# The first expert product as seven half-size products on half chunks of 256 columns, with the sums of the tokens kept

## The chip, the cores and the metric

The kernel runs on one core of a Trainium2 chip. The metric is the device time of one execution in microseconds. The core has engines that run side by side, each with its own queue in program order: TensorE (PE, matrix products into PSUM banks), VectorE (DVE) and ScalarE (ACT), which read PSUM, GpSimd (POOL), which here works in SBUF, and SyncE (SP), which issues the transfers.

## The reference

Three layers in float32: attention with a sink and a window, a dense mixture of eight experts, and a feed-forward layer.

```
x = attention(q, k, v)                       # 1536 tokens x 512
P = exp(x @ w_gate - max)                    # 1536 x 8 experts
for _ in range(8):
    P /= P.sum(1) + 1e-9;  P /= P.sum(0) + 1e-9;  P *= N / E
out = sum over e of P[:, e] * (relu(x @ w1[e]) @ w2[e])     # 512 -> 1024 -> 512
y = relu(out @ w_in) ** 2 @ w_out            # 512 -> 2048 -> 512
```

## The kernel before

Every float32 operand is split into a high and a low part (`xh` and `xl`, `wh` and `wl`), both in the rounded format that the matmuls read, and a product is three matmuls: high by low, high by high, low by high. The depth of 512 is four slices of 128.

The experts' hidden columns are cut into chunks of 512: chunks 0 to 15 are the eight experts (two each), chunks 16 to 19 the feed-forward layer. Chunk 0 fills TensorE's gaps in the attention phase (`phase_a`), with 384 tokens to a matmul. From chunk 1 on (`phase_b`) a chunk is taken for three blocks of 512 tokens. For each block come four groups of the first product (`mm1`, L452: 12 matmuls, weights stationary, 512 tokens as columns), each followed by a relu into `hh` on ScalarE (L464) and by the low part `hl` on VectorE (L465); then the four groups of the second product (`mm2`, L500) of the block before, one for each 128 tokens, each followed by an accumulation in `acc` on VectorE, scaled with the expert's column of P (L518; L513 and L515 without a scale). An engine's order is the order of the code: `phase_b` records a group, then its evacuation, then one step of the side work.

Side work is the splitting of the next chunk's weights (high part on ScalarE L390, low part on GpSimd L391), and the gate, a generator of half steps. A half step normalises P by rows (four small VectorE operations, L582 to L585) or by columns (a matmul with ones on TensorE, L590, and four operations, L594 to L600). The weights of the feed-forward layer come as 64-bit floats and are converted by eight VectorE operations per piece of 512 (L401 to L424, in four steps); 8 pieces of a chunk are spread over the 24 groups of the chunk before, one step to a group. Ahead of chunk 16 the accumulated tokens are transposed back (`x2`: L528 on TensorE, `xh` on ScalarE L534, `xl` on VectorE L535).

Of the kernel before, what the change touches and what calls it, by code (L numbers as in the profile page):

```python
# [19 lines left out]
NT = B * S  # L20
# [14 lines left out]
QKW = (QW + KW[0], QW + KW[1])  # L35
BIG = 1e30
# [3 lines left out]
class Kernel:  # L40
# [8 lines left out]
    def pool(self, ctx, name, bufs=1, space=None):  # L49
        if space:  # L50
            return ctx.enter_context(self.tc.tile_pool(name=name, bufs=bufs, space=space))
        return ctx.enter_context(self.tc.tile_pool(name=name, bufs=bufs))
# [311 lines left out]
    def w_load(self, c, which, half=0):  # L364
        src = (self.w1, self.w2)[which][c]
        pool = self.wraw[self.wk % len(self.wraw)]
        self.wk += 1
        if c < NC1:
            raw = pool.tile([128, KD, FC], F32, tag="wraw", name="wraw")
        else:  # L370
            raw = pool.tile([128, KD // 2, FC, 2], I32, tag="wraw", name="wraw64")
            s = slice(half * KD // 2, (half + 1) * KD // 2)
            src = src[:, s].bitcast(I32).rearrange("p k (f t) -> p k f t", t=2)
        self.nc.sync.dma_start(out=raw, in_=src)
        self.wr[c, which, half] = raw

    def w_split(self, c, which, piece, n=4):

        nc = self.nc
        if piece == 0:  # L380
            pool = self.wp[c % 2]
            nm = f"w{which}_{c % 2}"
            self.W[c, which] = tuple(
                pool.tile([128, KD, FC], F32R, tag=nm + t, name=nm + t) for t in "hl"
            )
        hi, lo = self.W[c, which]
        s = slice(piece * KD // n, (piece + 1) * KD // n)
        if c < NC1:
            src = self.wr[c, which, 0][:, s]
            nc.scalar.activation(out=hi[:, s], in_=src, func=AF.Copy)  # L390
            nc.gpsimd.tensor_tensor(  # L391
                out=lo[:, s], in0=src, in1=hi.bitcast(F32)[:, s], op=ALU.subtract
            )
            return

        raw, k = self.wr[c, which, piece // 2], piece % 2
        h, l = raw[:, k, :, 1], raw.bitcast(U32)[:, k, :, 0]
        x, m = (self.rp.tile([128, FC], I32, tag=t, name=t) for t in ("cx", "cm"))
        sg = self.rp1.tile([128, FC], I32, tag="cs", name="cs")
# [7 lines left out]
            out=sg, in0=h, scalar1=-0x80000000, scalar2=None, op0=ALU.bitwise_and  # L407
# [10 lines left out]
            out=x, in0=x, scalar=23, in1=sg, op0=ALU.logical_shift_left, op1=ALU.bitwise_or  # L418
# [7 lines left out]
        nc.scalar.activation(out=hi[:, piece], in_=mf, func=AF.Copy)  # L426
        nc.gpsimd.tensor_tensor(
            out=lo[:, piece], in0=mf, in1=hi.bitcast(F32)[:, piece], op=ALU.subtract
        )
# [8 lines left out]
    def mm1(self, ps, c, t0, n, f):  # L438
        nc = self.nc
        if f == 0:  # L440
            pool = self.hp[0 if n == QW else self.hk % 2]
            self.hk += 1
            self.h[c, t0] = tuple(
                pool.tile([128, KD, 512], F32R, tag="h" + t, name="h" + t) for t in "hl"
            )
        w1h, w1l = self.W[c, 0]
# [12 lines left out]
    def mm1_evac(self, c, t0, n, f, ps):  # L459
# [9 lines left out]
        else:  # L469
            r = self.rp.tile([128, 512], F32, tag="r", name="r")  # L470
            gq = self.rp.tile([128, 512], F32, tag="gq", name="gq")
# [5 lines left out]
            self.late = gq, hh, hl, f  # L477

    def finish(self):

        if self.late:
            gq, hh, hl, f = self.late
            nc = self.nc
            nc.scalar.activation(out=hh[:, f, :], in_=gq, func=AF.Copy)
            nc.vector.tensor_tensor(
                out=hl[:, f, :], in0=gq, in1=hh.bitcast(F32)[:, f, :], op=ALU.subtract
            )
            self.late = None
# [18 lines left out]
    def mm2_evac(self, c, t0, n, t, ps):  # L507
        nc = self.nc
        ti = t0 // 128 + t
        a = self.acc[:, ti, :]  # L510
        self.finish()
        if c in (0, NC1):
            nc.vector.tensor_copy(out=a, in_=ps)  # L513
        elif c == 1 or c > NC1:
# [6 lines left out]
        if c == NC1 + NC2 - 1:  # L521
            nc.sync.dma_start(out=self.out[ti * 128 : (ti + 1) * 128, :], in_=a)
# [17 lines left out]
    def gate(self):  # L540
        nc, g = self.nc, self.gp
        pt = self.mmtile()
        for b in range(3):
# [7 lines left out]
            lg = self.rp.tile([16, 512], F32, tag="r", name="lg")  # L551
# [55 lines left out]
    def moe_groups(self, first):  # L607

        if first == 1:
            for t0 in range(0, NT, QW):  # L610
                for f in range(FC // 128):
                    yield ("1", 0, t0, QW, f)
                for t in range(QW // 128):
                    yield ("2", 0, t0, QW, t)
        blocks = [(c, t0, 512) for c in range(first, NC1 + NC2) for t0 in range(0, NT, 512)]
        for k, (c, t0, n) in enumerate(blocks):
            for f in range(FC // 128):
                yield ("1", c, t0, n, f)
            if blocks[k + 1 : k + 2] and blocks[k + 1][0] == NC1:
                for kc in range(KD):  # L620
                    yield ("x", c, *blocks[k + 1][1:], kc)
            if k:
                for t in range(4):
                    yield ("2", *blocks[k - 1], t)
        for t in range(4):
            yield ("2", *blocks[-1], t)

    def group(self, gr):

        kind, c, t0, n, i = gr  # L630
        if kind == "x":
            self.x2(t0 // 512, i)
            return
# [11 lines left out]
    def filler(self, gen):  # L645

        for gr in gen:
            if gr[1] > 0:
                self.next = gr
                return  # L650
# [4 lines left out]
    def run(self):  # L655
# [17 lines left out]
        with ExitStack() as all_:  # L673
            self.reset()
            self.wp = [self.pool(all_, "wp0"), None]
            self.hp = [self.pool(all_, "hp0"), None]
            self.wraw = [self.pool(all_, "wraw0")]
            with tc.manual_schedule():
                gen = self.moe_groups(1)
                with ExitStack() as actx:  # L680
                    self.att = self.pool(actx, "att")
# [7 lines left out]
                    fill = self.phase_a(gen)  # L689
                self.phase_b(all_, 1, fill, gen)  # L690
        with tc.If(nc.values_load(self.flag, min_val=0, max_val=1)):
            with ExitStack() as all_:
                self.reset()
                with tc.manual_schedule():
# [5 lines left out]
                    self.wp = [self.pool(all_, "gwp0"), None]  # L700
                    self.hp = [self.pool(all_, "ghp0"), None]
                    self.wraw = [self.pool(all_, "gwraw0")]
                    gen = self.moe_groups(0)
                    self.phase_b(all_, 0, None, gen)

    def reset(self):
        self.mmk = self.hk = self.wk = 0
# [102 lines left out]
    def phase_a(self, gen):  # L810
# [27 lines left out]
        for u in range(U + 4):  # L838
# [35 lines left out]
            for i in [i for i, x in enumerate(W_AT) if x == u]:  # L874
                for _ in self.w_split(0, *divmod(i, 4)):
                    pass
# [4 lines left out]
    def phase_b(self, ctx, c0, fill, gen):  # L881
        nc = self.nc
        self.wp[1] = self.pool(ctx, f"wp1{c0}")
        self.wraw.append(self.pool(ctx, f"wraw1{c0}"))
        self.wk = 1
        self.hp[1] = self.pool(ctx, f"hp1{c0}")
        self.rp = self.pool(ctx, f"rp{c0}", 2)
        self.rp1 = self.pool(ctx, f"rp1{c0}")
# [3 lines left out]
        wg = self.pool(ctx, f"wg{c0}")  # L892
        self.wgz = wg.tile([128, KD, 128], F32R, name="wgz")
        wgr = wg.tile([128, KD, E], F32, name="wgr")
        nc.gpsimd.memset(self.wgz.bitcast(F32), 0.0)
        self.ones = wg.tile([128, 128], F32, name="ones")
        nc.gpsimd.memset(self.ones, 1.0)
        nc.sync.dma_start(out=wgr, in_=self.wg)
        events = {}
        loads = []  # L900
        for c in range(c0, NC1 + NC2):
            for which in range(2):
                for half in range(1 if c < NC1 else 2):
                    loads.append((c, which, half))
                for piece in range(4):
                    if c == 0:
                        at = (0, 0)
                    elif c == c0:
                        at = (which, piece)
                    else:  # L910
                        k = 4 * which + piece
                        at = (c - 1, {c0 + 1: 3 + 2 * k, NC1 + 1: 3 * k}.get(c, 1 + 3 * k))
                    events.setdefault(at, []).append(("split", c, which, piece))
        for piece in range(4):
            events.setdefault((2, 9 + piece), []).append(("scale", piece))
        loads.reverse()
        for _ in range(2):
            self.w_load(*loads.pop())
        h = self.wgz[:, :, 0:E]
# [131 lines left out]
```

## Time and profile before

| | before |
|---|---|
| median of 3 runs | 1485.55 us (1484.77 to 1487.75) |
| profiled execution: time, span | 1482.95 us, 1481.1 us |
| TensorE busy | 1448.7 us, 98% |
| VectorE busy | 679.6 us, 46% |
| ScalarE busy | 376.2 us, 25% |
| GpSimd busy | 278.5 us, 19% |
| mean granted clock of TensorE | 0.995 |

The time of an execution holds the span of the instructions and 1.85 us around it. A duration in a view is that of one instruction; neighbours on an engine can overlap a little, so the distance between two starts is what a queue pays.

### The profile page before, as it was taken

What the parts mean: (1) busy time and instruction counts of PE and PEld (TensorE: products, weight loads), DVE (VectorE), ACT (ScalarE), POOL (GpSimd) and SP (SyncE); (2) the same over time, 40 slices, a digit from 0 to 9 for tenths busy, and PEclk for the clock granted to TensorE, in tenths of its full rate; (3) what the DMA queues carried; (4) which work ended last, traced back from release to release, by engine and by line L of the source; (5) the groups of instructions that cost most, each with busy time, mean ns of one, the idle gap of its engine ahead of it and who ended that gap; (6) DMA issues with size and microseconds to landing.
All of it is one profiled execution on the core that took longest, in us unless ns stands there. A gap on an engine that the chain in (4) does not pass through costs nothing.

```text
span 1481.1 us, 16715 instructions
## 1 busy us (share of the span) xinstructions
PE 1448.7 (98%) x6791; PEld 1201.6 (81%) x6791; DVE 679.6 (46%) x1373; ACT 376.2 (25%) x807; POOL 278.5 (19%) x238
## 2 busy tenths in 40 slices
PE   5899999999999999999999999999999999999998
PEld 4688887888888888888888888888888888888887
DVE  7988836242222222222222222222223789688832
ACT  5767622111111211111121111112111133232221
POOL 4543312111111211111111111111110112011100
PEclk9899999999999999999999999999999999999999
DMA  3323121000001000000100000010000122011001
GB/s 111 116 61 94 35 86 57 29 29 29 29 29 58 29 29 29 29 29 29 58 29 29 29 29 29 29 58 27 30 29 29 57 86 84 30 58 58 29 22 66
DMA packets 15045, 67.76 MB, mean 46 GB/s; under 512 B 2160, under 2 KB 4208, under 8 KB 8816
## 3 DMA queue, kind: packets, MB, share of 16 engines
q1 hardware_dynamic: 14672, 66.61, 13.5%
q8 instruction: 55, 0.90, 0.3%
q14 instruction: 30, 0.25, 0.1%
q10 hardware_dynamic: 288, 0.00, 0.0%
HBM read 63.46 MB, written 3.15 MB: 45 GB/s over the span
## 4 chain that ended last, share of the span: by engine, by line
PE 93%; DVE 5%; ACT 1%; DMA 0%; issue 0%; ACTq 0%; DVEq 0%
PE mm L500 44%; PE mm L452 43%; PE xp L348 3%; PE sc L220 1%; DVE p L260 1%; PE ptp L273 1%; DVE p L233 1%; DVE st L250 1%; DMA wn_i<-window 0%; ACT qkh L175 0%; DVE ptl L309 0%; PE mm L547 0%; DVE hl L465 0%; ACT p L243 0%; PE mm L528 0%; DVE rs L583 0%
## 5 line engine op out<-in xcount | busy, mean ns | idle before, releaser
L464 ACT ACTIVATE hh<-mm 128x512 fp32r<-128x512 f32 (+1 forms) x196 | 115.3, 588 | 795.5 <-PE mm L452 795.5
L465 DVE SCALAR_TENSOR_TENSOR hl<-mm,hh 128x512 fp32r<-128x512 f32 (+1 forms) x196 | 133.3, 680 | 373.5 <-ACT hh L464 373.5
L518 DVE SCALAR_TENSOR_TENSOR acc<-mm,P,acc 128x512 f32<-128x512 f32 x168 | 125.9, 750 | 279.0 <-PE mm L500 279.0
L452 PE MATMUL mm<-xl,w_0h 128*128 128x512 f32 (+1 forms) x496 | 191.1, 385 | 0.0
L452 PE MATMUL mm<-xh,w_0h 128*128 128x512 f32 (+1 forms) x496 | 190.6, 384 | 0.0
L452 PE MATMUL mm<-xh,w_0l 128*128 128x512 f32 (+1 forms) x496 | 189.7, 382 | 0.0
L500 PE MATMUL mm<-w_0h,hh 128*128 128x512 f32 x480 | 187.7, 391 | 0.0
L500 PE MATMUL mm<-w_0l,hh 128*128 128x512 f32 x480 | 187.5, 391 | 0.0
L452 PE MATMUL mm<-xh,w_1l 128*128 128x512 f32 x480 | 187.2, 390 | 0.0
L500 PE MATMUL mm<-w_1h,hl 128*128 128x512 f32 x480 | 187.1, 390 | 0.0
L500 PE MATMUL mm<-w_0h,hl 128*128 128x512 f32 x480 | 186.9, 389 | 0.0
L452 PE MATMUL mm<-xh,w_1h 128*128 128x512 f32 x480 | 186.8, 389 | 0.0
L500 PE MATMUL mm<-w_1l,hh 128*128 128x512 f32 x480 | 186.8, 389 | 0.0
L500 PE MATMUL mm<-w_1h,hh 128*128 128x512 f32 x480 | 186.7, 389 | 0.0
L452 PE MATMUL mm<-xl,w_1h 128*128 128x512 f32 x480 | 186.7, 389 | 0.0
L391 POOL TENSOR_TENSOR w_1l<-wraw,w_1h 128x512 fp32r<-128x512 f32 x64 | 81.8, 1287 | 427.3 <-ACT w_1h L390 427.3
L391 POOL TENSOR_TENSOR w_0l<-wraw,w_0h 128x512 fp32r<-128x512 f32 x64 | 81.5, 1282 | 361.9 <-ACT w_0h L390 359.3
L452 PEld LDWEIGHTS mm<-xl,w_0h 128*128 128x128 f32 x496 | 93.1, 188 | 18.5 <-issue 1.3
L452 PEld LDWEIGHTS mm<-xh,w_0h 128*128 128x128 f32 x496 | 93.1, 188 | 18.3 <-issue 1.1
L452 PEld LDWEIGHTS mm<-xh,w_0l 128*128 128x128 f32 x496 | 93.1, 188 | 16.8
L500 PEld LDWEIGHTS mm<-w_0h,hh 128*128 128x128 f32 x480 | 90.1, 188 | 19.3 <-issue 0.7
L500 PEld LDWEIGHTS mm<-w_0l,hh 128*128 128x128 f32 x480 | 90.1, 188 | 19.2 <-issue 0.7
(144 smaller groups left out, 1913.7 us busy)
## 6 DMA issues: line engine op xcount, KB each, us to landing
wraw<-w SPq DMA_DIRECT2D x32, 1024.0 KB, 4.9
wraw<-win SPq DMA_DIRECT2D x8, 1024.0 KB, 5.0
wraw<-wout SPq DMA_DIRECT2D x8, 1024.0 KB, 5.3
raw<-qkv SPq DMA_DIRECT2D x8, 624.0 KB, 3.9
raw<-qkv SPq DMA_DIRECT2D x8, 464.0 KB, 3.5
out<-acc SPq DMA_DIRECT2D x12, 256.0 KB, 2.0
vraw<-qkv SPq DMA_DIRECT2D x8, 256.0 KB, 2.7
vraw<-qkv SPq DMA_DIRECT2D x8, 192.0 KB, 2.4
```

What stands on the lines that cost most here:

```text
L220: nc.tensor.matmul(out=ps[:, 0:wd], lhsT=x[r, l * 128 : (l + 1) * 128], rhs=y[r, QW + off : QW + off + wd], start=(m == 0), stop=(m == 2),)
L233: self.nc.vector.tensor_tensor_reduce(out=p[:, a, 0:wd], in0=self.sc[u][a][:, 0:wd], in1=mask[a], scale=-(D ** -0.5), scalar=3e38, op0=ALU ...
L250: self.nc.vector.tensor_scalar(out=st, in0=st, scalar1=1e-9, scalar2=None, op0=ALU.add)
L260: self.nc.vector.tensor_scalar(out=p[:, a, 0:wd], in0=p[:, a, 0:wd], scalar1=st[:, 2 + a : 3 + a], scalar2=None, op0=ALU.mult,)
L273: nc.tensor.transpose(ps[:, a, j * 128 : (j + 1) * 128], p[:, a, tt[a] + j * 128 : tt[a] + (j + 1) * 128], self.ident,)
L348: nc.tensor.matmul(out=o, lhsT=l, rhs=r, start=(k == 0), stop=(k == last), skip_group_check=True)
L391: nc.gpsimd.tensor_tensor(out=lo[:, s], in0=src, in1=hi.bitcast(F32)[:, s], op=ALU.subtract)
L452: nc.tensor.matmul(out=ps[:, 0:n], lhsT=w[:, kc, f * 128 : (f + 1) * 128], rhs=x[:, kc, t0 : t0 + n], start=(k == 0), stop=(k == 3 * KD - 1),)
L464: nc.scalar.activation(out=hh[:, f, 0:n], in_=ps[:, 0:n], func=AF.Relu)
L465: nc.vector.scalar_tensor_tensor(out=hl[:, f, 0:n], in0=ps[:, 0:n], scalar=0.0, in1=h32[:, f, 0:n], op0=ALU.max, op1=ALU.subtract,)
L500: nc.tensor.matmul(out=ps, lhsT=x[:, f, s], rhs=w[:, f, :], start=(k == 0), stop=(k == 3 * KD - 1),)
L518: nc.vector.scalar_tensor_tensor(out=a, in0=ps, scalar=self.P[:, ti, e : e + 1], in1=a, op0=ALU.mult, op1=ALU.add)
```

## The change

From half chunk 2 on (i = 2c + h, 256 hidden columns each) the expert layer goes through phases (i, pair), where a pair is half of the tokens: two quarters of 384. For i of 4 and more, `fast_phase` takes the first product as a 2 x 2 block product in Winograd's form of Strassen's scheme: blocks of two depth slices, 128 columns and 384 tokens, seven products p1 to p7 of 6 matmuls (L701) where plain blocks would need eight. The operands are single blocks or sums of blocks: S1 to S4 of the weights, made for each half chunk on GpSimd (L419) and split like the rest, and T1 to T4 of the tokens, made once (`sums`, L629 and L642) and kept; T1 overwrites one block in place (`late`) when chunk 1 is done. The products are put together by five additions on VectorE (L745), a copy on ScalarE (L751), and accumulation of some products in one PSUM bank. Then come relu (L682) and low part (L685). Half chunks 2 and 3 run `plain_phase`, the same blocks without the scheme. The second product is six groups of 6 matmuls with 512 columns (`half_mm2`, L793), each with an accumulation (`add_up`, L599 to L604), interleaved with the products of the next phase. `run` takes an entry (a product or a group), then one step of side work, then a half step of the gate, which now starts in phase (2,0). The 64-bit weights (`wide_split`, L477 to L500, `wide_part`) are converted from phase (31,0) on, four pieces there at one step to an entry, the pieces of later chunks at two steps to an entry.

```diff
+    def sums(self, pair):
...
+        def diff(a, b, kc, tag):
+            x = tt("q", f32(a, 0, kc), f32(b, 0, kc), ALU.subtract)
+            y = tt("s", f32(a, 1, kc), f32(b, 1, kc), ALU.subtract, nc.gpsimd)
+            return tt(tag, x, y, ALU.add)
+
+        def from_(a, t, kc, tag):
+            x = tt(tag, f32(a, 0, kc), t, ALU.subtract)
+            nc.vector.tensor_tensor(out=x, in0=x, in1=f32(a, 1, kc), op=ALU.add)
+            return x
...
+        def early():
+            for kc in range(2):
+                t1 = diff("B12", "B11", kc, "u")
+                yield
+                t2 = from_("B22", t1, kc, "z")
+                put("T2", kc, t2)
+                yield
+                put("T4", kc, from_("B21", t2, kc, "q"))
+                yield
+                put("T3", kc, diff("B22", "B12", kc, "q"))
+                yield
+
+        def late():
+            for kc in range(2):
+                put("T1", kc, diff("B12", "B11", kc, "u"))
+
+        return early(), late
...
+    def products(self, ps, jobs, start=True):
+
+        n = 6 * len(jobs)
+        k = 0
+        for (wh, wl), (xh, xl) in jobs:
+            for kc in range(2):
+                for w, x in ((wh, xl), (wh, xh), (wl, xh)):
+                    self.nc.tensor.matmul(
+                        out=ps, lhsT=w[:, kc], rhs=x[:, kc], start=start and k == 0,
+                        stop=(k == n - 1), skip_group_check=True,
+                    )
+                    k += 1
...
+    def fast_phase(self, i, pair):
+
+        nc = self.nc
+        v = {}
+        UNITS = {"A11": (0, 0), "A12": (0, 1), "A22": (0, 2),
...
+
+        def mul(bank, a, b, first):
+            if first:
+                v[bank] = self.mmtile()[:, 0:QW]
+            g, k = UNITS[a]
+            w = tuple(x[:, k] for x in self.W[i, 0][g : g + 2])
+            self.products(v[bank], [(w, self.operand(b, pair))], start=first)
+            self.finish()
+
+        def tt(name, tag, a, b):
+            v[name] = self.scratch2(tag)
+            nc.vector.tensor_tensor(out=v[name], in0=v[a], in1=v[b], op=ALU.add)
+
...
+            self.half_tiles(i, pair)
+            mul("a", "A11", "B11", True)
+            v["s"] = self.scratch2("s")
+            nc.scalar.activation(out=v["s"], in_=v["a"], func=AF.Copy)
+
+        def p6():
+            mul("b", "S2", "T2", True)
+            tt("u", "u", "b", "s")
+
+        def p2():
+            mul("a", "A12", "B21", False)
+            self.to_h(i, pair, 0, 0, v["a"])
+
+        def p5():
+            mul("c", "S1", "T1", True)
+            tt("z", "z", "c", "u")
+
+        def p7():
+            mul("d", "S3", "T3", True)
+            tt("c22", "q", "d", "z")
+            self.to_h(i, pair, 1, 1, v["c22"])
+
+        def p3():
+            mul("c", "S4", "B22", False)
+            tt("c12", "q", "c", "u")
+            self.to_h(i, pair, 0, 1, v["c12"])
+
+        def p4():
+            mul("d", "A22", "T4", False)
+            tt("c21", "q", "d", "u")
+            self.to_h(i, pair, 1, 0, v["c21"])
+
+        return [p1, 0, p6, p2, 1, p5, 2, p7, 3, p3, 4, p4, 5]
...
+    def half_mm2(self, i, pair):
+
+        def group(tile_):
+            def go():
+                t, s = tile_ // 3, slice(tile_ % 3 * 128, (tile_ % 3 + 1) * 128)
+                hh, hl = self.h[i, pair][t]
...
+                k = 0
+                for f in range(2):
+                    for x, w in ((hh, wh), (hh, wl), (hl, wh)):
+                        self.nc.tensor.matmul(
+                            out=ps, lhsT=x[:, f, s], rhs=w[:, f], start=(k == 0), stop=(k == 5)
+                        )
+                        k += 1
+                self.finish()
+                self.add_up(i // 2, 6 * pair + tile_, ps, i == 0)
+            return go
+        return [group(t) for t in (3, 4, 5, 0, 1, 2)]
 
     def x2(self, b, kc):
...
+        def run(seq, prev, steps=1):
+            for g in seq:
+                if isinstance(g, int):
+                    if g >= len(prev):
+                        continue
+                    g = prev[g]
+                g()
+                for _ in range(steps):
+                    side_step()
+                next(gate, None)
...
+        for i in range(i0, 2 * NC1):
+            for pair in range(2):
+                seq = (self.fast_phase if i >= FAST else self.plain_phase)(i, pair)
...
+                    self.wide_load(wide.pop())
+                    todo += [self.wide_part(k, wide) for k in range(4)]
+                elif i + 1 < 2 * NC1:
+                    load()
+                    todo.append((self.half_w1, self.half_w2)[pair](i + 1))
+                if (i, pair) in ((FAST - 2, 1), (FAST - 1, 0)):
+                    todo.append(sums[1 - pair][0])
+                if i == 4:
+                    todo.insert(0, scale(pair))
+                run(seq, prev)
+                prev = self.half_mm2(i, pair)
...
+                    while pair == 1 and todo or sums[0][0] in todo:
+                        side_step()
+                    sums[pair][1]()
+            while todo:
...
+        for c in range(NC1, NC1 + NC2):
+            if c + 1 < NC1 + NC2:
+                k = 8 * (c + 1 - NC1)
+                todo += [self.wide_part(k + j, wide) for j in range(8)]
+            for b in range(NT // 512):
+                seq = []
+                for f in range(FC // 128):
+                    seq.append(self.whole(("1", c, 512 * b, 512, f)))
+                    if c == NC1 and b + 1 < NT // 512:
+                        seq.append(self.x2_group(b + 1, f))
+                run(seq + [0, 1, 2, 3], prev, 2)
+                prev = [self.whole(("2", c, 512 * b, 512, t)) for t in range(4)]
+        run([0, 1, 2, 3], prev)
+        assert not todo
...
```

TensorE, in the middle of an expert chunk, before: where a block's last group of the first product (w_0h and w_0l are its weights' parts) meets the second product of the block before. Each group has 12 rows.

```order
L452 MATMUL mm<-xl,w_0h 128x512
L452 MATMUL mm<-xh,w_0h 128x512
L452 MATMUL mm<-xh,w_0l 128x512
...
L500 MATMUL mm<-w_0h,hh 128x512
L500 MATMUL mm<-w_0l,hh 128x512
L500 MATMUL mm<-w_0h,hl 128x512
```

After, at the products p7 (token sum T3 in Th and Tl) and p3 in a fast phase, with a group of the phase before between them (g4h and g4l are the parts of the weight sums):

```order
L701 MATMUL mm<-Tl,g4h 128x384
L701 MATMUL mm<-Th,g4h 128x384
L701 MATMUL mm<-Th,g4l 128x384
...
L793 MATMUL mm<-w2h,hh 128x512
L793 MATMUL mm<-w2l,hh 128x512
L793 MATMUL mm<-w2h,hl 128x512
...
L701 MATMUL mm<-xl,g4h 128x384
L701 MATMUL mm<-xh,g4h 128x384
L701 MATMUL mm<-xh,g4l 128x384
```

Groups are now 6 rows long, those of the first product with 384 columns, and the two products alternate.

VectorE in the gate, before: two half steps, with the evacuation of one group between them.

```order
L582 TENSOR_REDUCE rs<-P 128x12
L583 TENSOR_SCALAR rs<-rs 128x12
L584 RECIPROCAL rs<-rs 128x12
L585 TENSOR_TENSOR P<-P,rs 128x96
L513 COPY acc<-mm 128x512
L594 TENSOR_REDUCE cs<-mm 128x8
```

After, in phase (2,1), with a part of the token sums:

```order
L878 SCALAR_TENSOR_TENSOR P<-P,cs 128x96
L601 TENSOR_TENSOR acc<-mm,acc 128x512
L629 TENSOR_TENSOR tq<-xh 128x384
L629 TENSOR_TENSOR tq<-tq,ts 128x384
L860 TENSOR_REDUCE rs<-P 128x12
L861 TENSOR_SCALAR rs<-rs 128x12
L862 RECIPROCAL rs<-rs 128x12
L863 TENSOR_TENSOR P<-P,rs 128x96
L685 SCALAR_TENSOR_TENSOR hl<-mm,hh 128x384
L872 TENSOR_REDUCE cs<-mm 128x8
```

Between an evacuation (L601, L685) and the half step of the gate stand the two operations of a sum's part, and the entries between half steps are half as long.

VectorE in the feed-forward layer, before: one step of a 64-bit piece to a group.

```order
L474 SCALAR_TENSOR_TENSOR gq<-mm,r 128x512
L410 TENSOR_SCALAR cx<-cx 128x512
L413 TENSOR_SCALAR cm<-cm 128x512
L485 TENSOR_TENSOR hl<-gq,hh 128x512
L474 SCALAR_TENSOR_TENSOR gq<-mm,r 128x512
L417 SCALAR_TENSOR_TENSOR cx<-cx,cs 128x512
```

After, in chunk 16, where a group of the first product and a transpose alternate:

```order
L813 TENSOR_TENSOR xl<-mm,xh 128x512
L477 TENSOR_SCALAR cx<-raw_11286 128x512
L481 TENSOR_SCALAR cm<-raw_11286 128x512
L482 TENSOR_SCALAR raw_11286<-raw_11286 128x512
L486 TENSOR_SCALAR cx<-cx 128x512
L489 TENSOR_SCALAR cm<-cm 128x512
L556 TENSOR_TENSOR hl<-gq,hh 128x512
L550 SCALAR_TENSOR_TENSOR gq<-mm,r 128x512
L493 SCALAR_TENSOR_TENSOR cx<-cx,raw_11286 128x512
L496 SCALAR_TENSOR_TENSOR cm<-raw_11286,cm 128x512
L500 TENSOR_TENSOR cm<-cm,cx 128x512
L813 TENSOR_TENSOR xl<-mm,xh 128x512
```

A whole piece, all eight operations, now stands between the `xl` (L813) of one transpose and that of the next.

## Rows read from the trace of the kernel before

**Rows 1.** The page, part 1: busy time and share of each engine.

```profile
PE 1448.7 (98%) x6791; PEld 1201.6 (81%) x6791; DVE 679.6 (46%) x1373; ACT 376.2 (25%) x807; POOL 278.5 (19%) x238
```

**Rows 2.** The chain that ended last, in order of time: start us, us, what.

```profile
273.88 10.88 PE mm L500 x48
...
1443.35 10.88 PE mm L452 x48
```

**Rows 3.** Windows, columns PE, PEld, DVE, ACT, POOL, PEclk, DMA share, GB/s.

```profile
400.00:800.00 400.00, 400.00 (x1766) 331.24 (x1765) 106.36 (x148) 70.24 (x124) 63.72 (x50) 1.00 0.10 32
1188.00:1260.00 72.00, 72.00 (x343) 60.35 (x342) 66.54 (x123) 24.65 (x46) 15.74 (x11) 1.00 0.24 80
```

**Rows 4.** The same chain, around the last groups with 384 columns.

```profile
191.58 2.82 PE mm L500 x12
...
206.46 2.09 PE mm L452 x12
```

**Rows 5.** Timeline of TensorE, a group with 384 columns beside attention.

```profile
75.60 0.33 PE L452 MATMUL mm<-xh,w_0h 128*128 128x384 f32 x1
...
76.48 0.34 PE L452 MATMUL mm<-xl,w_0h 128*128 128x384 f32 x1
```

**Rows 6.** Groups by form, weight loads of TensorE.

```profile
L452 PEld LDWEIGHTS mm<-xh,w_0h 128*128 128x128 f32 x496 | 93.1, 188 | 18.3 <-issue 1.1
```

**Rows 7.** Groups by form, VectorE: shapes, count | busy us, mean ns | idle before.

```profile
L518 DVE SCALAR_TENSOR_TENSOR acc<-mm,P,acc 128x512 f32<-128x512 f32 x168 | 125.9, 750 | 279.0 <-PE mm L500 279.0
...
L465 DVE SCALAR_TENSOR_TENSOR hl<-mm,hh 128x384 fp32r<-128x384 f32 x16 | 8.8, 551 | 10.7 <-ACT hh L464 10.7
L358 DVE TENSOR_TENSOR xl<-xp,xh 128x384 fp32r<-128x384 f32 x16 | 8.7, 546 | 5.2 <-ACT xh L357 5.2
...
L583 DVE TENSOR_SCALAR rs<-rs 128x12 f32<-128x12 f32 x8 | 5.6, 702 | 0.3
...
L598 DVE TENSOR_SCALAR cs<-cs 128x8 f32<-128x8 f32 x8 | 3.0, 378 | 0.3
```

**Rows 8.** Timeline of VectorE, a piece of 64-bit weights among other work.

```profile
1195.47 0.91 DVE L410 TENSOR_SCALAR cx<-cx 128x512 int32<-128x512 int32 x1
1196.31 0.42 DVE L413 TENSOR_SCALAR cm<-cm 128x512 f32<-128x512 int32 x1
...
1197.24 0.68 DVE L417 SCALAR_TENSOR_TENSOR cx<-cx,cs 128x512 int32<-128x512 int32 x1
1197.84 0.68 DVE L420 SCALAR_TENSOR_TENSOR cm<-wraw,cm 128x512 f32<-128x512 uint32 x1
...
1199.71 2.05 DVE L518 SCALAR_TENSOR_TENSOR acc<-mm,P,acc 128x512 f32<-128x512 f32 x3
1201.68 0.43 DVE L401 TENSOR_SCALAR cx<-wraw 128x512 int32<-128x512 int32 x1
1202.03 0.41 DVE L405 TENSOR_SCALAR cm<-wraw 128x512 int32<-128x512 int32 x1
```

**Rows 9.** Timeline of VectorE, one half step of the gate.

```profile
222.94 0.24 DVE L582 TENSOR_REDUCE rs<-P 128x12 f32<-128x96 f32 x1
223.22 0.17 DVE L583 TENSOR_SCALAR rs<-rs 128x12 f32<-128x12 f32 x1
...
223.69 0.26 DVE L585 TENSOR_TENSOR P<-P,rs 128x96 f32<-128x96 f32 x1
```

**Rows 10.** Waits of TensorE for VectorE in the gate.

```profile
PE mm L590 <- DVE P L585: 2.8, 5, 1.2
```

**Rows 11.** Groups by form, ScalarE and GpSimd.

```profile
L464 ACT ACTIVATE hh<-mm 128x384 fp32r<-128x384 f32 x16 | 7.7, 480 | 6.3 <-PE mm L452 6.3
...
L391 POOL TENSOR_TENSOR w_1l<-wraw,w_1h 128x512 fp32r<-128x512 f32 x64 | 81.8, 1287 | 427.3 <-ACT w_1h L390 427.3
...
L190 POOL TENSOR_TENSOR vl<-vraw,vh 128x384 fp32r<-128x384 f32 x8 | 8.0, 1001 | 21.9 <-ACT vh L189 21.9
```

**Rows 12.** The page, part 6: DMA issues, KB each, us to landing.

```profile
wraw<-w SPq DMA_DIRECT2D x32, 1024.0 KB, 4.9
```

More of the change, by code (lines that the diff above doesn't have):

```diff
@@ L361, in att_x @@
         )
[L364 to L375, printed above, removed]
@@ new lines, in half_w2, with wide_load @@
+    def half_w2(self, i):
+        raw = self.wr.pop((i, 1))
+        w = tuple(
+            self.w2p[i % 2].tile([128, 2, FC], F32R, tag="w" + t, name="w2" + t) for t in "hl"
+        )
+        self.W[i, 1] = w
+        for k in range(2):
+            self.pair_split(w[0][:, k], w[1][:, k], raw[:, k])
+            yield
+    def wide_load(self, k):
+        c, which, piece = k // 8, k // 4 % 2, k % 4
+        raw = (self.late_p, self.sp)[k % 2].tile([128, FC, 2], I32, tag="s", name="raw64")
+        src = (self.w1, self.w2)[which][NC1 + c][:, piece].bitcast(I32)
+        self.nc.sync.dma_start(out=raw, in_=src.rearrange("p (f t) -> p f t", t=2))
+        self.wr[k, 2] = raw
@@ L895, in phase_b @@
         nc.gpsimd.memset(self.wgz.bitcast(F32), 0.0)
-        self.ones = wg.tile([128, 128], F32, name="ones")
+        self.ones = self.wg_p.tile([128, 128], F32, name="ones")
         nc.gpsimd.memset(self.ones, 1.0)
         nc.sync.dma_start(out=wgr, in_=self.wg)
[L899 to L919, printed above, removed]
-        nc.scalar.activation(out=h, in_=wgr, func=AF.Copy)
+        todo = [self.half_w1(i0), self.half_w2(i0)]
+        def side_step():
+            while todo:
+                try:
+                    return next(todo[0])
+                except StopIteration:
+                    todo.pop(0)
@@ L948, in after, with scale @@
-        def after():
-            self.evac()
-            next(gate, None)
-        if fill:
-            before(0)
-            for _ in fill:
-                if self.done:
-                    after()
-                    before(0)
-            after()
-            gen = itertools.chain([self.next], gen)
-        for gr in gen:
-            before(gr[1] if gr[0] != "2" else max(count))
+        sums = [self.sums(p) for p in range(2)]
+        def scale(pair):
+            for ti in range(6 * pair, 6 * pair + 6):
+                nc.vector.tensor_scalar(
+                    out=self.acc[:, ti, :], in0=self.acc[:, ti, :],
+                    scalar1=self.P[:, ti, 0:1], scalar2=None, op0=ALU.mult,
+                )
+                yield
@@ L962, in phase_b, with whole, go, x2_group @@
+        run([0, 1, 2, 3], prev)
+        assert not todo
+        left.close()
+    def whole(self, gr):
+        def go():
             for _ in self.group(gr):
                 pass
-            after()
-        assert not events and not ends, events
+            self.evac()
+        return go
+    def x2_group(self, b, kc):
+        return lambda: self.x2(b, kc)
+    def wide_part(self, k, wide):
+        for j, _ in enumerate(self.wide_split(k)):
+            if j == 2 and wide:
+                self.wide_load(wide.pop())
+            yield
```

378 lines of the change are left out of this document (259 added, 119 removed).

## The prediction

> **What bounds the kernel now.** I read the page's busy shares first: TensorE works 98% of the span, VectorE 46%, ScalarE 25%, GpSimd 19% [rows 1]. The chain that ended last says what that is made of: from 263 us on nothing but blocks of 48 matmuls, 10.88 us each, alternately of the first product (L452) and the second (L500) [rows 2]. That is 10.88 / 48 = 0.2267 us per matmul of 512 columns, without a gap; the windows say the same (400.00 us busy in 400 us, with VectorE at 106.36) [rows 3]. The reader should see that in this stretch only fewer or shorter matmuls can gain, and that whatever makes TensorE wait is a pure loss. The one place where VectorE is also nearly full is where the 64-bit weights are converted: 66.54 of 72 us, TensorE still at 72.00 [rows 3].
>
> **What is removed on TensorE.** Chunks 2 to 15 change from 144 matmuls of 512 columns to 4 phases (two half chunks by two token pairs) of 7 products of 6 matmuls with 384 columns, 168 in all. The second product keeps its number of 512-column matmuls. All hangs on the price of a 384-column matmul in a full stream. The trace has them only between attention work: 2.09 us for 12, that is 0.174, in the chain where a group of 12 with 512 columns takes 2.82 [rows 4], and 0.176 in the timeline (76.48 - 75.60 over five) [rows 5]. Bounds: by columns alone 0.75 x 0.2267 = 0.170; from above the weight load of 188 ns that each matmul has beside it [rows 6], if loads could not overlap one another. I take 0.1745, because rows 4 and 5 are the very shape and were run with those loads.
>
> Per chunk 144 x 0.2267 = 32.64 becomes 168 x 0.1745 = 29.32; 14 chunks save **46.6 us** (57.2 at 0.170, 14.9 at 0.188). The Trainium skill (TensorE: Matmul & The Clock Gate, section Back-to-back issue gap) gives N/2.4 + 2.5 ns, 215.8 and 162.5 ns here; rows 2 and 4 lie 11 to 12 ns above it for the two sizes, and by the page the saving would be an estimated 52.8 us. Chunk 1, which is only re-cut (192 matmuls of 384 for 144 of 512), costs 192 x 0.1745 - 32.64 = **+0.9**.
>
> **What is added in a steady phase.** A fast phase lasts TensorE 42 x 0.1745 + 36 x 0.2267 = 15.5 us. VectorE now recombines: 5 additions (L745), 4 low halves (L685), 6 accumulations (L604; twice as many as L518, since each group now sums half of the depth). Listed durations overlap: 0.68 us ops follow each other at 0.60, the accumulations at (1201.68 - 1199.71) / 3 = 0.66 [rows 8], so I price 384-column ops (listed 0.551 and 0.546 [rows 7]) at 0.47: 9 x 0.47 + 6 x 0.66 = 8.2 us of 15.5 (9.5 by listed durations). Each product has another group of 1.05 to 1.36 us between it and its reader. The closest dependence is p2, which adds into the bank that ScalarE must first copy (0.48 [rows 11]): p6 and a second-product group, 2.4 us, cover that. GpSimd splits the weights and makes their sums: 512 elements take 1.28, 384 take 1.00 [rows 11], so 256 about 0.72; four sums and seven low halves are 7.9 us in the fuller of two phases. Weights are prepared a half chunk ahead. So this work costs nothing while VectorE is less than about 1 us behind; if the cover were gone, each late result would cost up to 1.1 us in each of 56 phases. Loads are the same bytes in halves, landing in at most the 4.9 us of the whole ones [rows 12]. The first ones now wait for attention's buffers (191.6), but are needed only after the logits, about 206 [rows 4]: nothing.
>
> **What it costs at the head.** The gate was spread over groups of 2.1 to 2.8 us [rows 4]; TensorE waited for its normalised P 2.8 us in all [rows 10]. Now it advances in entries of 1.36 (second-product group) or 2.1 us, and the kept token sums stand in the same VectorE queue between an evacuation and the gate, as the order shows. One half step of the gate: 1.0 us from its reduce to its multiply's end in [rows 9], with the mean 702 ns of the slow add instead of 170 (and 378 for the other half [rows 7]) 1.5 and 1.2. In phase (2,1), the second pair of half chunk 2, TensorE has 4 x 2.1 + 6 x 1.36 = 16.6 us, VectorE 10 x (0.57 + 1.35) + 8 x 0.94 = 26.7. The ones-matmul of the gate stands in TensorE's order, so it can't run ahead: **+10** here, against 2.8 before. In (3,0) to (4,0) come the sums of the second pair, the in-place T1 and the scaling; GpSimd takes 2 x 1.00 per T1 part (difference, then low half) with one buffer, two such parts and four scalings at 0.66 are ahead of the z that p3 needs: about 4 + 2.6 = **+6.6**, the roughest term. Net head 13.8, range 5 to 20.
>
> **What it costs at the tail.** One converted piece takes VectorE, by the pitches of [rows 8], 3 x 0.34 + (0.84 + 0.34) + 2 x 0.60 + 0.60 = 4.0 us. Before, each of 24 groups of 2.72 us carried one of its four steps. Now four pieces lie in phase (31,0), one step per entry: 8.2 + 13 = 21 us of VectorE against 15.5, which surfaces as late halves and sums (1.35 + 1.1), a last accumulation that the first transpose waits for (2.2) and the next transposes (1.7): 6.4. Then chunk 16 takes two steps per entry. A first-product group and a transpose group are 2.72 + 0.44 = 3.16 us on TensorE, but on VectorE 2 x 0.60 + 0.60 + 4.0 = 5.8. Over four pairs VectorE falls 4 x 2.64 = 10.6 us behind, and the first group of the next 512 tokens needs xl of the last transpose: about 11.5 with the rest of the queue. **+18**, range 9 to 24 (9 if a third of the steps find idle time; 24 if the accesses that make L410 0.84 instead of 0.34 hit the other steps too). The four second-product groups behind let VectorE catch up, so nothing follows.
>
> **Sum:** -46.6 + 0.9 + 13.8 + 18 = -13.9. The profiled execution took 1482.95 us (span 1481.1), so 1469; it lies 2.6 below the median of 1485.55, on whose scale the forecast is **1471**.
>
> **Rivals.**
> 1. The stalls are mostly hidden: VectorE's ops find gaps that my queue walk doesn't see, as before, where 66.54 busy of 72 cost TensorE nothing [rows 3]. With none left, 1485.55 - 46.6 + 0.9 - 2.8 = 1437; with half of them, 1454. Against it: TensorE runs in order, and both stretches ask for more VectorE time than they last.
> 2. Slower: a product of 384 columns can't hide its weight load in an unbroken stream and takes 188 ns [rows 6]. Then the saving is 14.9, and with head, tail and chunk 1 the sum is +17.8: 1503. The prices meet where the saving is 32.7, at 0.1804 us a matmul; a wait of 13.9 / 56 = 0.25 us in each fast phase decides as well. Against it: rows 4 and 5, 0.174 to 0.176 beside the same loads.
> 3. Head and tail each at their upper ends (20 and 24): -46.6 + 0.9 + 44 = -1.7, 1484: no change that can be told.
>
> **How the numbers follow.** Forecast 0.66 (1458 to 1483), rival 1 0.14 (1437 to 1458), rival 3 0.08 (1481 to 1487), rival 2 0.12 (above 1487). Range 1450 to 1488: leaves out half of rival 1 and most of rival 2. A difference under 0.2%, 3 us, can't be told from none here. Faster: most of the forecast and rival 1, 0.81; same 0.08; slower 0.11.
>
> **What the changed profile would show.** Right: rows of the chain with L701 x6 at 1.05 us and L793 x6 at 1.36, windows in 350 to 1150 with TensorE fully busy and VectorE near 53 to 60%; idle TensorE of about 17 us between 215 and 265, released by gate P and by the z of L745; about 18 between 1135 and 1190, released by low halves, accumulations and xl. Wrong: L701 rows at 1.12 or more (rival 2), TensorE idle regularly in each phase with L745, L685 or the L751 copy as releaser, or windows at head and tail without idle time (rival 1).

## The result and the profile after

The changed kernel took 1505.10 us (median of 4 runs, 1503.52 to 1505.81) beside 1485.16 of the kernel before (4 runs as well): the ratio is 1.0132 with a 95% interval of 1.0113 to 1.0151. It is slower, where 1471 was forecast, with a range of 1450 to 1488. The profiled execution has a span of 1501.7 us against 1481.1, 20.6 more. The page, part 1, of the changed kernel:

```profile
PE 1422.9 (95%) x7175; PEld 1244.0 (83%) x7175; DVE 999.7 (67%) x1933; ACT 459.2 (31%) x1083; POOL 455.7 (30%) x523
```

Against [rows 1] TensorE is busy for 25.8 us less, and yet ends later: it is idle for longer. The windows say where (columns as in [rows 3]):

```profile
240.00:265.00 25.00, 15.23 (x76) 12.52 (x74) 23.36 (x56) 4.10 (x8) 8.42 (x9) 1.00 0.06 21
265.00:290.00 25.00, 20.43 (x105) 18.21 (x105) 18.65 (x44) 5.57 (x14) 11.96 (x16) 1.00 0.07 22
290.00:340.00 50.00, 36.13 (x167) 31.34 (x166) 31.38 (x55) 12.69 (x29) 28.09 (x29) 0.86 0.05 17
340.00:1140.00 800.00, 800.00 (x4000) 721.45 (x3999) 475.72 (x771) 213.01 (x489) 268.52 (x337) 1.00 0.10 34
...
1180.00:1220.00 40.00, 34.89 (x163) 28.49 (x162) 36.93 (x68) 9.20 (x17) 6.07 (x4) 0.96 0.16 53
1220.00:1260.00 40.00, 27.44 (x117) 21.19 (x116) 39.52 (x67) 12.85 (x24) 8.07 (x6) 0.79 0.25 79
```

The reader sees three parts: a head with 9.8 + 4.6 + 13.9 = 28.2 us of idle TensorE, 800 us without any, and a tail in which VectorE (39.52 of 40) is the full engine. The chain that ended last, at these places:

```profile
245.71 0.18 DVE rs L860
...
246.38 1.07 DVE P L863
...
296.03 1.01 POOL xl L398
...
319.12 0.02 ACT xh L397
319.14 0.41 issue
319.55 0.48 ACT ts L751
320.03 0.04 issue
320.07 2.29 PE mm L701 x6
322.36 2.46 PE mm L793 x6
324.82 1.04 PE mm L701 x6
325.87 1.39 PE mm L793 x6
...
1055.05 2.08 PE mm L701 x12
...
1117.49 2.08 PE mm L701 x12
...
1148.74 2.10 PE mm L701 x12
...
1221.66 0.68 DVE xl L813
...
1222.68 1.45 DVE cm L481
...
1228.30 0.68 DVE xl L813
...
1268.23 0.70 DVE xl L813
1268.97 9.13 PE mm L527 x39
1278.10 10.88 PE mm L578 x48
```

The pieces L701 x12 are p6 and p2, once a phase, so 1055.05 to 1117.49 are four phases of 15.61 us. A chunk takes 62.44 instead of 288 x 0.2267 = 65.29. The largest waits of TensorE outside attention (us in total, times, longest):

```profile
PE mm L868 <- DVE P L863: 14.3, 6, 3.2
PE mm L701 <- ACT ts L751: 13.5, 2, 11.8
PE mm L527 <- DVE xl L813: 13.5, 4, 5.0
...
PE mm L806 <- DVE acc L604: 2.4, 2, 1.9
```

The gate's wait answers to [rows 10], where it was 2.8; the other three are new. Against the forecast's own terms:

| term | forecast | measured | how |
|---|---|---|---|
| fast phases, 14 chunks | -46.6 | -39.9 | 14 x (62.44 - 65.29) |
| head | +13.8 | +27.7 | 28.2 idle, less 2.8 before, and 2.3 of slow clock behind the wait (2.29 + 2.46 - 1.04 - 1.39) |
| tail | +18 | +27.8 | below |

For the tail, phase (31,0) would start at 1161.99, a phase of 15.61 behind (30,1), whose p6 stands at 1148.74. Up to 1278.10, where chunk 16's second block of the second product starts, there are 88.3 us of TensorE work: two phases, 12 transpose groups of 0.44, six second-product groups of 1.39, and 192 matmuls at 0.2267. 116.1 passed. With the 0.9 of chunk 1 the terms sum to +16.5 of the 20.6. Of the other 4 us, 1.4 lie in attention, which by the two chains ended at 192.95 instead of 191.58 us with the same matmuls (in the profiled executions of this case it ended between 190.8 and 196.2), and 0.9 behind the last matmul (6.0 us to the end of the span instead of 5.1). Some 2 us I could not place.

### The profile page after: what moved, and what is told of

Its sections match the earlier page's. It is cut to its first block, busy times and chain, and to the rows that moved or that the text cites. A ratio compares the mean times of both kernels' runs of the same rounds, so it can differ in the third digit from the quotient of the medians.

```text
span 1501.7 us, 18970 instructions
## 1 busy us (share of the span) xinstructions
PE 1422.9 (95%) x7175; PEld 1244.0 (83%) x7175; DVE 999.7 (67%) x1933; ACT 459.2 (31%) x1083; POOL 455.7 (30%) x523
## 4 chain that ended last, share of the span: by engine, by line
PE 82%; DVE 12%; ACT 2%; issue 2%; POOL 1%; DMA 1%; ACTq 0%; DVEq 0%; POOLq 0%; SPq 0%
PE mm L793 30%; PE mm L701 28%; PE mm L578 10%; PE mm L527 9%; PE xp L349 2%; PE sc L221 1%; DVE p L261 1%; PE ptp L274 1%; DVE cm L481 1%; DVE p L234 1%; DVE acc L604 1%; DVE cm L496 1%; DVE cx L493 1%; ACT qkh L176 1%; DVE xl L813 0%
## 5 line engine op out<-in xcount | busy, mean ns | idle before, releaser
L604 DVE SCALAR_TENSOR_TENSOR acc<-mm,P,acc 128x512 f32<-128x512 f32 x336 | 251.4, 748 | 135.0 <-PE mm L793 135.0
L793 PE MATMUL mm<-w2h,hh 128*128 128x512 f32 x720 | 284.2, 395 | 1.5 <-ACT hh L682 1.0
L793 PE MATMUL mm<-w2h,hl 128*128 128x512 f32 x720 | 283.7, 394 | 0.0
L793 PE MATMUL mm<-w2l,hh 128*128 128x512 f32 x720 | 283.4, 394 | 0.0
L682 ACT ACTIVATE hh<-tq 128x384 fp32r<-128x384 f32 x168 | 88.3, 525 | 433.5 <-DVE tq L745 433.5
L793 PEld LDWEIGHTS mm<-w2h,hl 128*128 128x128 f32 x720 | 135.7, 188 | 31.0 <-DVE hl L685 0.3
L685 DVE SCALAR_TENSOR_TENSOR hl<-tq,hh 128x384 fp32r<-128x384 f32 x168 | 94.0, 560 | 97.7 <-ACT hh L682 97.7
L793 PEld LDWEIGHTS mm<-w2h,hh 128*128 128x128 f32 x720 | 135.7, 188 | 18.4 <-ACT hh L682 1.3
L793 PEld LDWEIGHTS mm<-w2l,hh 128*128 128x128 f32 x720 | 135.8, 189 | 15.8
L701 PE MATMUL mm<-xl,g3h 128*128 128x384 f32 x272 | 92.7, 341 | 14.5 <-ACT ts L751 13.5
L701 PE MATMUL mm<-xh,g3l 128*128 128x384 f32 x272 | 91.7, 337 | 0.0
L701 PE MATMUL mm<-xh,g3h 128*128 128x384 f32 x272 | 91.6, 337 | 0.0
L527 PE MATMUL mm<-xl,v0h 128*128 128x512 f32 x192 | 77.1, 402 | 13.5 <-DVE xl L813 13.5
L682 ACT ACTIVATE hh<-mm 128x384 fp32r<-128x384 f32 x72 | 35.4, 491 | 166.9 <-PE mm L701 166.9
L685 DVE SCALAR_TENSOR_TENSOR hl<-mm,hh 128x384 fp32r<-128x384 f32 x72 | 40.1, 557 | 66.1 <-ACT hh L682 66.1
L701 PE MATMUL mm<-xl,g4h 128*128 128x384 f32 x240 | 81.3, 339 | 1.0 <-DVE tz L745 1.0
L701 PE MATMUL mm<-xh,g4h 128*128 128x384 f32 x240 | 80.6, 336 | 0.0
L701 PE MATMUL mm<-xh,g4l 128*128 128x384 f32 x240 | 80.5, 336 | 0.0
L701 PE MATMUL mm<-Tl,g4h 128*128 128x384 f32 x224 | 75.9, 339 | 0.6 <-DVE acc L601 0.6
```

Source lines behind the costliest of these rows:

```text
L527: nc.tensor.matmul(out=ps[:, 0:n], lhsT=w[:, kc, f * 128 : (f + 1) * 128], rhs=x[:, kc, t0 : t0 + n], start=(k == 0), stop=(k == 3 * KD - 1),)
L604: nc.vector.scalar_tensor_tensor(out=a, in0=ps, scalar=self.P[:, ti, e : e + 1], in1=a, op0=ALU.mult, op1=ALU.add)
L682: nc.scalar.activation(out=hh, in_=src, func=AF.Relu)
L685: nc.vector.scalar_tensor_tensor(out=hl, in0=src, scalar=0.0, in1=hh.bitcast(F32), op0=ALU.max, op1=ALU.subtract)
L701: self.nc.tensor.matmul(out=ps, lhsT=w[:, kc], rhs=x[:, kc], start=start and k == 0, stop=(k == n - 1), skip_group_check=True,)
L793: self.nc.tensor.matmul(out=ps, lhsT=x[:, f, s], rhs=w[:, f], start=(k == 0), stop=(k == 5))
```

## The experiments

All are edits of the changed kernel. "Against changed" is the difference of the ratios times 1485.5.

| run | median us | ratio to before (95%) | against changed |
|---|---|---|---|
| changed | 1505.10 | 1.0132 (1.0113 to 1.0151) | |
| e1 scheme from half chunk 6 | 1511.04 | 1.0165 (1.0146 to 1.0184) | +4.9 |
| e2 plain products | 1525.96 | 1.0272 (1.0255 to 1.0290) | +20.8 |
| e3 tail spread | 1493.66 | 1.0055 (1.0036 to 1.0073) | -11.4 |
| e4 low half on VectorE | 1506.77 | 1.0147 (1.0130 to 1.0164) | +2.2 |
| e5 other buffer | 1506.19 | 1.0143 (1.0127 to 1.0160) | +1.6 |
| e6 difference on VectorE | 1503.13 | 1.0122 (1.0100 to 1.0144) | -1.5 |
| e7 6, VectorE, tail | 1490.31 | 1.0035 (1.0021 to 1.0050) | -14.4 |
| e8 5, VectorE, tail | 1488.24 | 1.0022 (1.0010 to 1.0034) | -16.3 |
| e9 no burst | 1502.40 | 1.0114 (1.0097 to 1.0130) | -2.7 |
| e10 no burst, VectorE, tail | 1488.77 | 1.0028 (1.0015 to 1.0042) | -15.4 |
| e11 no burst, 6, VectorE, tail | 1486.32 | 1.0008 (0.9997 to 1.0019) | -18.4 |
| e12 no burst, 5, earlier sums | 1470.97 | 0.9891 (0.9874 to 0.9907) | -35.8 |

**Is the scheme worth what its matmuls say?** e2 has `FAST = 40`. Expected:

> All half chunks in plain form (eight products of 6 matmuls, no sums, no recombination), the rest as in the changed kernel. Theory (in its 56 steady phases the scheme is worth what its matmuls say, 6 x 0.1745 = 1.05 us a phase, and VectorE and GpSimd cost nothing there): +58.6 us, less the stalls at the head that the sums cause (28 us down to about 4), so about 1505 + 59 - 24 = 1540 us, with the tail as it is. Rival (the recombination and the weight sums slow the steady phases down, so that the scheme is worth little): 1485 to 1500 us.

It came out at 1526. In its chain a plain phase is the distance between equal pieces two pairs of groups apart:

```profile
702.15 2.12 PE mm L701 x12
...
718.83 2.12 PE mm L701 x12
...
735.40 2.08 PE mm L701 x12
```

That is 16.68 and 16.57, 1.0 more than 15.61: 56 phases give 57 us, as the theory said. The rival is out. The total rose by only 21, 14 less than expected, since the plain kernel also has smaller stalls: the gate's wait is 3.9 and there is no wait for ts, so that TensorE is idle for 3.9 us at the head where the changed kernel had 28.2. At the tail, where (31,0) has no recombination beside the conversion, it is idle for 15.6 where that had 19.9.

**The tail.** e3 changes rates alone (`run` carries the fraction of a step on to the next entry):

```diff
...
-                run(seq, prev)
+                run(seq, prev, 0.63 if i == 2 * NC1 - 1 else 1)
...
-        run(steps[0:2] + [0, steps[2], 1, steps[3], 2, 3, 4, 5], prev)
+        run(steps[0:2] + [0, steps[2], 1, steps[3], 2, 3, 4, 5], prev, 0.5)
...
-                run(seq + [0, 1, 2, 3], prev, 2)
+                run(seq + [0, 1, 2, 3], prev, 1 if c == NC1 else 2)
```

> Only the rate of the 64-bit conversion is changed: 0.63 steps to an entry in half chunk 31, 0.5 ahead of chunk 16, 1 in chunk 16, 2 from chunk 17 on as before. Theory (about 29 us are lost between the start of (31,0) and the second product in chunk 16 because the steps crowd VectorE's queue ahead of what TensorE waits for): two thirds of the crowd's steps have room elsewhere, so 10 to 18 us less, 1487 to 1495. Rival (VectorE is short of time over the whole stretch, wherever the steps stand): within 3 us of 1505.

11.4 us less, with TensorE's wait for xl down from 13.5 to 2.8, and 321.9 us instead of 333.9 from the first matmul of (31,0) to the last of all: the steps had room elsewhere, and their place is the cause of that part. e4 takes GpSimd out of the conversion:

```diff
-        self.pair_split(hi[:, piece], lo[:, piece], mf)
+        nc.scalar.activation(out=hi[:, piece], in_=mf, func=AF.Copy)
+        nc.vector.tensor_tensor(
+            out=lo[:, piece], in0=mf, in1=hi.bitcast(F32)[:, piece], op=ALU.subtract
+        )
```

> The low half of a converted 64-bit piece is made by VectorE (one more operation of 0.60 us) instead of GpSimd. Theory (L481 takes 1.45 us instead of 0.41 because it meets GpSimd's low half of the piece before, and VectorE's queue is the path from 1202 to 1269 us): L481 falls back to 0.41 or so, each piece on the path takes 1.04 - 0.60 = 0.44 us less, about 12 pieces, so -5 us: 1500. Rival (L481 is slow for itself or for its load): each piece takes 0.60 more, 1512 us.

The mechanism was right and the gain was not. It came out at 1506.77. All 32 executions of L481 are now alike (ns min/median/max):

```profile
L481 DVE TENSOR_SCALAR cm<-raw x32: 418/421/427, 1168.6 to 1405.6; 128x512 int32<-128x512 int32 x32
```

But VectorE's queue now holds the low half, 0.69 us, which takes back most of what L481 saves: in chunk 16 a pair of groups takes 6.3 us of VectorE instead of 6.6. From the first matmul of (31,0) to the last of all 332.6 us pass instead of 333.9, 1.3 less where 5 were expected, and the total can't be told from the changed kernel's.

**The head: the gate.** e1 has `FAST = 6`, so that the sums stand behind the gate.

> The scheme starts at half chunk 6 instead of 4, so the sums of the tokens are made in (4,1) and (5,0), after the gate has ended. Theory (TensorE's 28 us of idle time between 215 and 321 us come from the gate, the sums and their scratch buffers standing in the same queues at the same time): two more half chunks in plain form cost 4 x 1.05 = +4.2 us, the gate's waits fall from 14.3 us to about 4, and the wait for the copy ts (11.8 us) at least halves, so about 1505 + 4 - 10 - 6 = 1493 us. Rival (the sums are work that TensorE waits for wherever it stands): the idle time moves with them, 1509 us.

The gate's wait fell from 14.3 to 3.9 as the theory had it, but the wait for ts stayed at 13.5 and 8.7 us of waits for hl came with the sums, which had only moved. As a whole, at 1511.04, the rival was nearer.

**The head: the wait for ts.** e5 (the first line added below) writes ts to z's buffer, e6 (the second) makes it on VectorE:

```diff
-            y = tt("s", f32(a, 1, kc), f32(b, 1, kc), ALU.subtract, nc.gpsimd)
+            y = tt("z", f32(a, 1, kc), f32(b, 1, kc), ALU.subtract, nc.gpsimd)
+            y = tt("s", f32(a, 1, kc), f32(b, 1, kc), ALU.subtract)
```

> The difference of the low parts (ts) in the sums of the tokens is written to the buffer of z instead of that of s, which p1's copy also needs. Buffer theory (TensorE's wait of 11.8 us for the copy ts in (4,0) is for the one buffer s, which the last T1 part holds to the end): the wait falls by 8 to 11 us, 1495 us. Chain theory (the sums go round GpSimd, VectorE and ScalarE, some 3.2 us a part, and TensorE needs u and z, which come behind the last part on VectorE): the wait only moves on to p6, p2 or p3; 0 to -3, 1503 us.

> The difference of the low parts is made by VectorE (0.57 us) instead of GpSimd (0.97 us), where it stands in line behind the low half of the part before, which waits for ScalarE. Chain theory: a part of the chain gets about 1.5 us shorter from 289 us on, where some ten parts are left; -8 to -12 us there, and VectorE's extra operation costs up to 2 us beside the gate: 1495 to 1499 us. Buffer theory: s is held as long as before, less only 0.4 us a part: 1502 us.

Both theories fell on e5: the wait of 11.8 us was neither shorter nor somewhere else. In e6 it fell only to 10.0, and the total, 1503.13 where 1495 to 1499 were expected, can't be told from the changed kernel's. What stands ahead of the copy is seen in ScalarE's timeline of the changed kernel (start us, us, instruction, idle before and its releaser):

```profile
310.63 1.14 ACT L397 ACTIVATE w2h<-raw 128x512 fp32r<-128x512 f32 x2
311.67 0.48 ACT L682 ACTIVATE hh<-mm 128x384 fp32r<-128x384 f32 x1
315.94 0.52 ACT L397 ACTIVATE xh<-tu 128x384 fp32r<-128x384 f32 x1 [3.80 <-DVE tu L629]
319.12 0.52 ACT L397 ACTIVATE xh<-tu 128x384 fp32r<-128x384 f32 x1 [2.65 <-DVE tu L629]
319.55 0.47 ACT L751 ACTIVATE ts<-mm 128x384 f32<-128x384 f32 x1
```

TensorE had finished p1 at 304.3 and p6 at 308.3. The copy of p1 (L751) is recorded behind the high halves of T1 (xh), each of which waits for a sum that comes round every 3 us; ScalarE sits idle 3.80 and 2.65 us in front of them, and the copy runs the moment they are through. p2 adds to the copied bank, and all of TensorE waits. By the order of the code these two high halves belong to the second pair's T1, which (4,0) doesn't read; the first pair's sums had ended at 297.0 (the xl of the chain above). So what TensorE waits for here is a place in ScalarE's queue, not data that it needs. e7 and e8 join e6 with the tail's rates and `FAST = 6` or `5`:

> Three edits at once: the scheme from half chunk 6 on, the low difference on VectorE, and the spread rates of the 64-bit conversion as in the tail run. Theory: gate's waits 3.9 us as with half chunk 6, the chain's 18 us of waits down to about 5, the tail 11.5 us better, 4.2 us more plain work: about 1505 - 10 - 13 - 11.5 + 4 = 1475 us, below the kernel before. Rival (the chain is as long wherever it stands and whoever makes the difference): 1498 us.

> As the run with half chunk 6, but from half chunk 5 on: the sums stand in (3,1) and (4,0), where the gate has ended but the 12 scalings also lie. Theory: 2.1 us less plain work than with 6, and up to 4 us more in waits for VectorE, so 1473 to 1478 us. Rival: as with 6 or above by the whole scaling, 8 us: 1483 us.

They came out at 1490.31 and 1488.24, both well above what was expected. The gate's wait is 3.9 in both, but ts is still waited for, 10.1 us in e7, and in e8

```profile
PE mm L701 <- ACT ts L751: 19.8, 1, 19.8
```

So the burst itself was taken away: `late` yields behind each part (with q buffers only), and nothing is drained that the next phase doesn't need. The split of the next half chunk's weights moves ahead of the sums in the side work.

```diff
...
-                if i == FAST - 1:
-                    while pair == 1 and todo or sums[0][0] in todo:
+                if (i, pair) == (FAST - 1, 0):
+                    while sums[0][0] in todo:
                         side_step()
-                    sums[pair][1]()
-            while todo:
+                if (i, pair) in ((FAST - 1, 1), (FAST, 0)):
+                    while sums[pair ^ 1][1] in todo:
+                        side_step()
+            while todo and i != FAST - 1:
                 side_step()
```

> Of the changed kernel only the recording of the sums' last parts is changed: T1's four parts and the rest of the second pair's sums are side steps, one to an entry, up to the end of (4,0)'s steps, instead of a burst at the ends of (3,0) and (3,1). Queue theory (the copy ts waits because ScalarE takes its instructions in order, and the high halves of the whole burst, each of them waiting for the chain, stand ahead of it): the wait for ts falls from 11.8 us to about 2, the clock's dip behind it goes too, -10 to -14 us: 1491 to 1495 us. Chain theory (the sums take their 3.2 us a part and are needed soon): the wait is spread over the entries, -2 to -4: 1502 us.

> As the run before, with the low differences on VectorE and the spread conversion at the tail. Queue theory: 1505 - 12 - 11.5 = 1481 us, with the gate's waits of 12 to 14 us left as the largest loss. Chain theory: 1489 us.

> No burst, scheme from half chunk 6, low differences on VectorE, spread tail. Queue theory: against the run with 6 and the burst (1490) the 14 us of waits for ts and hl between 340 and 380 fall to about 2, and the slow clock behind them goes: 1474 to 1478 us. Chain theory: 1487 us.

All three came out at what the chain theory gave (1502.40, 1488.77 and 1486.32). Yet the wait is not spread over the entries, as that theory had it, but is still one for the copy: e9 took the wait for ts from 13.5 to 10.6 only, e10 has 6.8 left, and e11 11.5. Steps one to an entry (1.4 to 2.1 us) are still issued faster than the chain of some 3 us a part runs, so that the backlog stands in the queues when the first fast phase comes, burst or not. e12 gives it time: the sums start in (3,0), one phase earlier than in e8 with the same `FAST`, so that all but the four T1 parts are issued before half chunk 4, a half chunk (33 us) ahead of the first fast phase, (5,0). On VectorE the last of them ends at 310 us.

```diff
-FAST = 4
+FAST = 5
...
-                yield
+                if ti % 2:
+                    yield
...
-                if (i, pair) in ((FAST - 2, 1), (FAST - 1, 0)):
-                    todo.append(sums[1 - pair][0])
+                if (i, pair) in ((FAST - 2, 0), (FAST - 2, 1)):
+                    todo.append(sums[pair][0])
...
```

> No burst, scheme from half chunk 5, the sums starting in (3,0) and two scalings to a step, low differences on VectorE, spread tail. Queue theory: 2.1 us less plain work than with 6, some 2 us more beside the last half steps of the gate: 1473 to 1478 us, faster than the kernel before by 0.5 to 0.8%. Chain theory: 1485 us.

1470.97 us, 1.1% faster than the kernel before. Its copy runs without a wait for the queue, 0.04 us behind the end of p1 at 333.78 (timeline of ScalarE):

```profile
333.82 0.49 ACT L755 ACTIVATE ts<-mm 128x384 f32<-128x384 f32 x1 [3.28 <-PE mm L705]
```

No wait for ts is left in its list; the largest ones outside attention are

```profile
PE mm L872 <- DVE P L867: 5.4, 6, 1.9
PE mm L810 <- DVE acc L604: 3.6, 2, 3.1
PE mm L527 <- DVE xl L817: 2.8, 2, 2.6
```

e8 and e12 have the same `FAST`, the same engine for ts and the same tail. They differ in when the sums, the scalings and the weight split are issued, and in the buffers of the T1 parts. That is worth 0.0131 x 1485.5 = 19.5 us. In the profiled executions TensorE's idle time between 195 and 420 us falls from 23.7 to 8.1: the 19.8 for ts go, and some 4 us of other waits come.

## Why the prediction was wrong

**What bounds, and the steady phases: right.** TensorE is fully busy over 800 us, a 384-column matmul costs 1.04 / 6 = 0.173 to 0.175, and e2 gives 1.0 us a phase. The term was mis-sized by 6.7 us: I priced the second product at the 0.2267 of long groups, but in groups of six between products it takes up to 1.39 / 6 = 0.232. The estimate by the formula of the Trainium skill (TensorE: Matmul & The Clock Gate, section Back-to-back issue gap), -52.8, was farther off than the rows' (-46.6). Rival 2 fell: its 1503 us lie near the measured time by luck, since its condition, 0.188 us a matmul, isn't met.

**The failed step is the pair of stalls, "+10" with "+6.6" at the head and "+18" at the tail.** The phases were right, though the stalls lie later than the stretches that I named (240 to 320 us instead of 215 to 265, and 1162 to 1269 instead of 1135 to 1190). Rival 3, "Head and tail each at their upper ends", came nearest in its mechanism, with upper ends too low (44 against 55). In detail:

- "+10" in the gate: 14.3 waited, on VectorE's order as foretold. Part of the miss is in the price of a half step: P's multiply (L863) takes 1.07 us beside GpSimd's work, where [rows 9] had 0.26, and a half step with it 246.38 + 1.07 - 245.71 = 1.7, where 1.5 and 1.2 were forecast.
- "+6.6, the roughest term", for "the z that p3 needs": the wrong wait, 1.0 us in all (L701 for the tz of L745). Queues were counted on VectorE and GpSimd, but ScalarE, 25% busy, was not walked. Its high halves of the sums stand ahead of p1's copy, and I had written of that copy that 2.4 us of cover suffice. That holds in the steady phases and fails at the first one: 11.8 us, and a slow clock behind it.
- "+18": 27.8. In chunk 16 a pair of groups takes 1228.30 - 1221.66 = 6.6 us of VectorE where 5.8 were forecast, since L481 is held 1.1 us. "The four second-product groups behind let VectorE catch up" failed too: the next block's first product waited again, until 1268.97.

The sums of the prediction hold, but for two slips that change nothing here: its terms give 1471.6, which rounds to 1472, and the forecast and rival 1 together have a chance of 0.80, not 0.81.

**How the cause is shown.** The tail by e3 (the same work in other places, -11.4). The gate's crowding by e1 and e2 (14.3 to 3.9). That the sums cause the wait for ts by e2, which has no sums and no such wait, and by e8 against e12. That they do it through ScalarE's queue by the timeline, with e5 against the buffer; no run took the copy alone out of that queue. Some 2 us above the terms stay open, and so does how much of the tail's 27.8 would be left with the best order; in e12 three waits of 3.6, 2.8 and 1.7 us remain there.

## What to carry to other kernels

A scheme that saves matmuls pays its saving out in every phase, but its one-time work can cost more than all of that: here 40 us were won and 55 lost in some 200 us at the two ends. Walk every engine's queue at the first phase that uses the new operands, the idle engines too: a chain over three engines runs at its latency, not at its busy share, and whatever is recorded behind it waits, even a half-microsecond copy. Issue such work early enough that its backlog has drained, and spread conversions by the time of the entries that they ride on, not one or two to each.

## What the runs showed of the hardware

Some VectorE operations whose data lie in SBUF are held by a GpSimd operation that is running, until that ends. In the changed kernel this L481 starts 0.11 us behind GpSimd's low half and ends 0.28 us behind its end (timelines of VectorE and of GpSimd):

```profile
1222.60 1.52 DVE L481 TENSOR_SCALAR cm<-raw 128x512 int32<-128x512 int32 x1
```

```profile
1222.49 1.35 POOL L398 TENSOR_TENSOR Tl<-cm,Th 128x512 fp32r<-128x512 f32 x1 [4.88 <-ACT Th L397]
```

Without the GpSimd operation (e4) it takes 0.42. In the changed kernel 15 of the 17 L481 that overlap a low half are held like this; in the other two the next operation, L482, takes 1.40 instead of 0.43. Not all operations are held: a reciprocal of the gate (L877) that starts within a GpSimd operation takes its 0.20 as without one, and the additions that read PSUM (L745) their 0.56. The Trainium skill (SBUF — State Buffer, section SBUF: two separate sides) says that the two engines share a pair of ports as an exclusive lock held for a whole instruction, and that the loser blocks; these rows agree. So each low half on GpSimd that meets such an operation costs VectorE's queue 1.52 - 0.42 = 1.1 us here.

After the wait of 11.8 us TensorE's matmuls of 384 columns follow each other at 2.29 / 6 = 0.38 us, then its 512-column ones at 0.41, and from 4.8 us behind the end of the wait at 0.173 and 0.232 again; the granted clock of the window from 290 to 340 is 0.86, a mix of the levels of 1.2 and 2.4 GHz. Here the dip cost 2.3 us on top of the wait. At the tail, where the granted clock is 0.79 from 1220 to 1260, VectorE was the path and the dip lies beside it.
